# Turning the first batch's tokens by pairs of heads, loading its states second, and keeping two instead of four unsplit first tiles

## The chip, the cores and the metric

The kernel runs on one core of a Trainium2 chip. The metric is the time of one execution on the device in microseconds (us). An execution with a profile gives a trace; its span is somewhat shorter than its time, which also holds what lies around it.

## The reference

Eight batches of tokens `x` (8 heads, 512 tokens, 64 values a head) and of states (8 heads, 32 states, 64 values) read each other by softmax attention; both results go through one feed-forward layer. All inputs are double-precision numbers of which the kernel reads the words it needs.

```python
scores = scale * x @ state.T                  # (8, 8, 512, 32): tokens read states
a = softmax(scores, over states);  xread = a @ state
a2 = softmax(scale * state @ x.T, over tokens);  sread = a2 @ x
x_ = concat(xread, sread)                     # 8 * (512 + 32) rows of 512
h = x_ @ w_in                                 # 512 x 2048
g = h * clip(h + 3, 0, 6) / 6
out = g @ w_out                               # 2048 x 512
```

## The kernel before

**Stages.** The hidden layer's 2048 columns are 16 tiles of 128; a sweep is 8 of them. The units of work are: batches 0 to 7 with the first 8 tiles, the state rows of all batches with both halves, then batches 0 to 7 again with the other 8 tiles. A unit has 8 steps, one for each hidden tile. A step's first product makes `h` of a tile (in `ps_h`), ScalarE and VectorE make `g` of it, and two steps later its second products add `g @ w_out` into four accumulators (`acc0` to `acc3`, one for each 128 tokens).

**The states inside the weights.** For the token rows, `xread @ w_in` is computed as `a @ (state @ w_in)`: `wprime` multiplies the states of a batch (`stT`, turned) with tiles of `w_in` (through `all_heads`) and gives `wp`; the first product then multiplies `wp` with the turned softmax weights `aT`.

**Split numbers.** A single-precision product runs as slow passes on TensorE. So operands are split into a high part that TensorE takes in its fast format and the rest (`hi`, `lo`), and three fast products stand for one (`product`, `split`). The split costs a cast on ScalarE and a subtraction on VectorE for each tile. For the first tiles of batch 0 (`plain`) neither `wp` nor `g` nor `w_out` is split: the products run in single precision, with `a_first` as the weights. What those tiles' `w_out` needs in split form for later batches is made later (`late_halves`).

**The start.** `load_x(0, ...)` brings batch 0's tokens and `load_state(0, ...)` its states. VectorE copies the tokens into `xb`, TensorE turns them (`take_in`), and ScalarE copies the result into `xT` (which lies in `w_in3`). `tokens_by_rows` puts the turned states into block form (`apart`), multiplies them with `xT` (`scores`), makes the softmax with tokens in rows (maximum, difference, Exp, sum, reciprocal, product), turns the weights on TensorE and copies them into `a_first`. `scores_by_columns` makes the same scores with states in rows for `sread`. While TensorE has nothing, transposes of the identity keep it busy (the `idle` of `Plan.issue`). Later batches come turned by another way: 16 loads of 32x16x32 blocks each (`load_turned`) and transposes on VectorE, in two halves that each need one of three `raw` buffers.

**Weights.** `weight` loads a tile (or two) of double-precision words into a `raw` or `early` buffer, casts its upper words on ScalarE (`upper`, into `tops`) and joins them with the lower ones on VectorE (`join`).

**What sets the order.** The code adds operations with reads, writes, costs and due times to a `Plan`; a table of numbers, `RANKS`, one for each operation, gives their priority. `Plan.order` simulates five queues with the costs and takes, at each point, the operation with the lowest rank among those that can start soon. The resulting order is fixed in the program: each engine and SyncE's load queue run their rows strictly one after another. So a row that waits holds up all rows behind it on its engine.

```python
plain = lambda k, c: k == 0 and c == 0        # tiles 0 to 3 of batch 0
at(3, halves_of_first, 3.5)
```

## Time and profile before

| | |
|---|---|
| time, median of 3 runs | 647.61 us (646.58 to 649.05) |
| the profiled execution | 647.05 us |
| its span | 645.3 us |
| granted TensorE clock, mean | 1.0 |
| TensorE busy | 634.2 us (98%) |
| VectorE busy | 508.3 us (79%) |
| ScalarE busy | 324.8 us (50%) |
| GpSimd busy | 18.4 us (3%) |
| moved by DMA | 73.09 MB, mean 113 GB/s |

The times in the profile count from the start of the span. A row of the order of time has its start, its duration, the engine (PE is TensorE, PEld its weight loads, DVE VectorE, ACT ScalarE, SP SyncE; SPq is the issuing of loads), the line, the operation with its output and inputs, and how many equal ones were merged. A single-precision product counts as two records. Line numbers are those of the kernel before; in the changed kernel the same code stands some 10 to 33 lines further down.

### The profile page before, as it was taken

How to read it: one execution, taken by the hardware profiler on the slowest of the kernel's cores; microseconds unless marked ns; L12 is line 12 of the kernel's file. 1: busy time of each engine (PE TensorE's matmuls, PEld its weight loads, DVE VectorE, ACT ScalarE, POOL GpSimd, SP SyncE). 2: the span in 40 equal slices, each digit the busy share in tenths (PEclk: the TensorE clock that was granted, in tenths of full speed). 3: DMA queues.
4: the chain of work that ended last, by engine and by line, in shares of the span. 5: the costliest groups of instructions: out<-in, count | busy, mean ns of one | idle time of the engine just before them, and what ended most of it. 6: DMA issues, size and time to landing. Idle time of an engine off the chain costs nothing.

```text
span 645.3 us, 11398 instructions
## 1 busy us (share of the span) xinstructions
PE 634.2 (98%) x4422; PEld 515.2 (80%) x4422; DVE 508.3 (79%) x931; ACT 324.8 (50%) x585; POOL 18.4 (3%) x22
## 2 busy tenths in 40 slices
PE   7999999999999999999999999999999999999997
PEld 6446767777777868778899878898989898998996
DVE  5989778987979859878478769878887888798673
ACT  4848444555546444546346446455445454455431
POOL 0000000000000000000000000000000000000000
PEclk9999999999999999999999999999999999999999
DMA  9976696986839569344104032242424232413143
GB/s 296 247 195 184 133 201 101 261 170 165 190 71 234 122 192 215 87 78 145 21 1 135 1 103 70 40 100 34 102 35 99 33 89 25 112 21 60 15 81 70
DMA packets 148686, 73.09 MB, mean 113 GB/s; under 512 B 124696, under 2 KB 134424, under 8 KB 148504
## 3 DMA queue, kind: packets, MB, share of 16 engines
q1 hardware_dynamic: 144664, 64.23, 39.5%
q0 software_dynamic: 3824, 7.87, 8.4%
q8 instruction: 35, 0.57, 0.4%
q10 hardware_dynamic: 144, 0.26, 0.1%
q14 instruction: 19, 0.16, 0.1%
HBM read 42.45 MB, written 26.21 MB: 106 GB/s over the span
## 4 chain that ended last, share of the span: by engine, by line
PE 86%; DMA 5%; SPq 4%; DVE 2%; ACT 2%; issue 0%; DVEq 0%; ACTq 0%
PE ps_h L998 27%; PE acc L998 27%; PE acc L1110 24%; PE ps_s L614 3%; DMA early<-in_moe_w_out_dram 2%; PE ps_h L614 2%; PE acc L1281 1%; SPq L601 1%; DMA raw<-in_x_dram 1%; SPq L569 1%; DMA raw<-in_moe_w_out_dram 1%; DMA early<-in_moe_w_in_dram 1%; PE ps_h L955 1%; PE ps_h L1213 1%; ACT tops L472 1%; SPq L534 0%
## 5 line engine op out<-in xcount | busy, mean ns | idle before, releaser
L998 PE MATMUL acc<-w_out_hi,g_hi 128*128 128x512 f32 x288 | 114.9, 399 | 0.6 <-ACT g_hi L383 0.6
L998 PE MATMUL acc<-w_out_lo,g_hi 128*128 128x512 f32 x288 | 112.5, 391 | 0.2 <-DVE w_out_lo L506 0.2
L998 PE MATMUL acc<-w_out_hi,g_lo 128*128 128x512 f32 x288 | 112.2, 390 | 0.0
L1249 ACT ACTIVATE g<-ps_h,three 128x512 f32<-128x512 f32 (+1 forms) x80 | 51.2, 645 | 76.9 <-PE ps_h L998 64.7
L1110 PE MATMUL acc<-w_out_hi,tmp 128*128 128x256 f32 x360 | 89.0, 284 | 0.0
L998 PE MATMUL ps_h<-aT_hi,wp_hi 128*128 128x512 f32 (+1 forms) x224 | 81.3, 363 | 0.1
L998 PE MATMUL ps_h<-aT_lo,wp_hi 128*128 128x512 f32 (+1 forms) x224 | 80.8, 361 | 0.0
L998 PE MATMUL ps_h<-aT_hi,wp_lo 128*128 128x512 f32 (+1 forms) x224 | 80.4, 359 | 0.0
L1233 ACT ACTIVATE G<-ps_h,three 128x512 f32<-128x512 f32 x64 | 44.2, 691 | 68.4 <-PE ps_h L998 66.5
L1252 DVE SCALAR_TENSOR_TENSOR g<-g,ps_h 128x512 f32<-128x512 f32 (+1 forms) x80 | 50.0, 629 | 36.3 <-ACT g L1249 35.6
L998 PEld LDWEIGHTS acc<-w_out_hi,g_hi 128*128 128x128 f32 x288 | 54.1, 188 | 19.2 <-issue 7.2
L1110 PEld LDWEIGHTS acc<-w_out_hi,tmp 128*128 128x128 f32 x360 | 66.6, 192 | 3.0 <-issue 1.7
L1110 PE MATMUL acc<-w_out_hi,g_hi 128*128 128x256 f32 x240 | 68.2, 284 | 0.0
L1110 PE MATMUL acc<-w_out_lo,g_hi 128*128 128x256 f32 x240 | 67.9, 283 | 0.0
L1110 PE MATMUL acc<-w_out_hi,g_lo 128*128 128x256 f32 x240 | 67.9, 283 | 0.0
L998 PEld LDWEIGHTS acc<-w_out_hi,g_lo 128*128 128x128 f32 x288 | 54.1, 188 | 11.9 <-DVE g_lo L384 0.4
L998 PEld LDWEIGHTS acc<-w_out_lo,g_hi 128*128 128x128 f32 x288 | 54.1, 188 | 11.3 <-DVE w_out_lo L506 0.7
L1235 DVE SCALAR_TENSOR_TENSOR G<-G,ps_h 128x512 f32<-128x512 f32 x64 | 43.7, 686 | 20.8 <-ACT G L1233 20.1
L384 DVE TENSOR_TENSOR g_lo<-g,g_hi 128x512 fp32r<-128x512 f32 (+1 forms) x72 | 45.2, 641 | 10.7 <-ACT g_hi L383 9.0
L383 ACT CAST g_hi<-g 128x512 fp32r<-128x512 f32 (+1 forms) x72 | 40.8, 583 | 22.8 <-DVE g L1252 14.9
L1110 PE MATMUL acc<-w_out_lo,tmp 128*128 128x256 f32 x180 | 50.9, 283 | 0.0
L1110 PEld LDWEIGHTS acc<-w_out_hi,g_hi 128*128 128x128 f32 x240 | 45.9, 191 | 4.7 <-issue 2.5
(148 smaller groups left out, 1177.5 us busy)
## 6 DMA issues: line engine op xcount, KB each, us to landing
out_dram<-ot SPq DMA_DIRECT2D x8, 1024.0 KB, 5.2
out_dram<-ot POOLq DMA_DIRECT2D x15, 512.0 KB, 6.0
raw<-in_x_dram SPq DMA_DIRECT2D x112, 64.0 KB, 3.1
xb<-in_x_dram SPq DMA_DIRECT2D x28, 256.0 KB, 4.3
raw<-in_moe_w_out_dram SPq DMA_DIRECT2D x11, 511.8 KB, 4.0
raw<-in_moe_w_in_dram SPq DMA_DIRECT2D x8, 511.0 KB, 4.4
raw<-raw SPq DMA_DIRECT2D x112, 32.0 KB, 2.0
early<-in_moe_w_in_dram SPq DMA_DIRECT2D x3, 1023.0 KB, 9.3
```

Source lines behind the costliest of these rows:

```text
L383: first = S_(cost, rank, lambda: nc.scalar.copy(hi(), src()), reads, [writes[0]], after)
L384: V(cost, rank, lambda: nc.vector.tensor_tensor(lo(), src(), hi().bitcast(F32), op=ALU.subtract), [*reads, writes[0]], [writes[1]])
L472: nc.scalar.copy(out[..., 1], top)
L569: nc.sync.dma_start(x_tile(b, read)[:, :, j, :], x_v[b, j])
L601: nc.sync.dma_start(t[rows, i].rearrange("t (a c) -> t a c", c=NS), x[b, 4 * g + 2 * i + u, :, k * NS : (k + 1) * NS].rearrange("(a t) c - ...
L614: nc.tensor.matmul(out[u][cols, :], made["stT", b][rows, cols], moving(q)[rows], start=True, stop=True,)
L998: nc.tensor.matmul(ps, l, r, start=start and k == 0, stop=stop and k == n - 1)
L1110: nc.tensor.matmul(out, left(a, l), right(b, r), start=p == 0 and z == 0 and y == 0, stop=p == FPS // 2 - 1 and y == 2, skip_group_check=True)
L1233: S_(0.68, n - 1.5, lambda: nc.scalar.activation(g(), by_pass(), AF.Relu, bias=three, scale=-1.0 if turned_sign(FPS + i) else 1.0), [ps], ...
L1235: V(0.63, n - 1.5, lambda: nc.vector.scalar_tensor_tensor(g(), g(), 6.0, by_pass(), op0=ALU.min, op1=ALU.mult), [ps], [g_key])
L1249: in_turn["g", n] = S_(cost + 0.05, rank, lambda: nc.scalar.activation(g(), bank(ps)[:, :width], AF.Relu, bias=three, scale=-1.0 if turned ...
L1252: V(cost, rank, lambda: nc.vector.scalar_tensor_tensor(g(), g(), 6.0, bank(ps)[:, :width], op0=ALU.min, op1=ALU.mult), [ps], [g_key])
```

## The change

Six edits, all in the first microseconds but the last:

1. Batch 0's tokens are loaded in four pieces of two heads (256 KB), not two of four heads. The copies, transposes and scores go by these pieces: the scores of heads 0 to 3 fill one bank and those of heads 4 to 7 the other, where the banks were halves of the tokens before. Each bank's softmax is finished by itself, with a sum and a reciprocal of its own.
2. Batch 0's states are loaded by one transfer with rows of 512 bytes (two states in a partition) where there were two with rows of 256 bytes, and it is second in the queue. TensorE turns them by four products with columns of the identity instead of one transpose.
3. Two first tiles of batch 0 stay unsplit instead of four. Tiles 2 and 3 are split in all of `wp`, `g` and `w_out` like the later ones.
4. The unsplit `wp` lies in a `tmp` buffer, the scores' Exp in the second half of `w_in2`; the halves of the first weights (`halves_of_first`) are due two steps earlier.
5. Costs in the plan: VectorE's and ScalarE's are taken by 0.98, turning of tokens at 0.7 instead of 0.92.
6. `RANKS` is a new table of 2594 numbers, and with it the order of all engines changes to the end.

`split_by_queue` is added but nothing calls it.

```diff
-189 379 188 282 281 288 283 88 289 90 342 86 341 91 343 87 345 279 291 67 85 278 280 327 287 276 286 335 285 274 273
...
     def V(cost, rank, do, reads=(), writes=(), after=()):
-        return plan.add("V", cost, rank, do, reads, writes, after)
+        return plan.add("V", 0.98 * cost, rank, do, reads, writes, after)
...
-    plain = lambda k, c: k == 0 and c == 0
+    PLAIN = 2
+    plain = lambda k, f: k == 0 and f < PLAIN
...
-        if k < FPC:
+        if k < PLAIN:
             late_halves.append(halves)
...
-            for u in range(NG):
-                nc.sync.dma_start(raw[:, u, :], st_v[b, :, :, u, :])
+            nc.sync.dma_start(raw, state[b].rearrange("h (m k) d -> (h m) k d", k=NG))
...
-        for g in range(NG):
-            hs = slice(g * HG, (g + 1) * HG)
+        load_state(0, rank)
+        for q in range(NQ):
+            hs = slice(q * NG, (q + 1) * NG)
             def load(hs=hs):
                 nc.sync.dma_start(raw()[:, hs], x[0, hs].rearrange("h (p j) d -> p h j d", j=J))
-            Q(rank, 524.288, load, writes=[(*raw_key, g)], pieces=512, late=0.6)
-            if g == 0:
-                load_state(0, rank)
...
+            Q(rank + 0.1 * q, 262.144, load, writes=[(*raw_key, q)], pieces=256, late=0.5)
             V(0.37, rank, lambda hs=hs: nc.vector.tensor_copy(x_tile(0)[:, hs], raw()[:, hs]),
-              [(*raw_key, q // 2)], [(*key, "q", q)])
+              [(*raw_key, q)], [(*key, "q", q)])
...
-            T(0.25, rank, lambda: nc.tensor.transpose(
-                bank(st)[:, :P], made["st_raw", b].rearrange("p u d -> p (u d)"), ident),
-                [("st_raw", b)], [st], after)
+            def turn_first():
+                for u in range(NG):
+                    out = bank(st)[u * D : (u + 1) * D, :P].rearrange("p (q m k) -> p q m k", q=NQ, k=NG)
+                    for k in range(NG):
+                        nc.tensor.matmul(
+                            out[..., k], made["st_raw", b][:, k],
+                            ident.rearrange("p (q u m) -> p q u m", q=NQ, u=NG)[:, :, u], start=True, stop=True)
+            T(0.5, rank, turn_first, [("st_raw", b)], [st], after)
...
-        def scores(k):
-            out = bank(ps[k]).rearrange("p (j u q n) -> p j q u n", j=J // 2, u=NG, n=NS)
-            for j in range(J // 2):
-                for q in range(NQ):
-                    js = slice((k * J // 2 + j) * P, (k * J // 2 + j + 1) * P)
+        def scores(q):
+            out = bank(ps[q // 2]).rearrange("p (j u q n) -> p j q u n", j=J, u=NG, n=NS)
+            for j in range(J):
                     nc.tensor.matmul(
...
+        for e, bt_key in enumerate(bt_keys):
...
+            V(0.6, -6.21, lambda m1=m1, src=src: nc.vector.tensor_reduce(m1(), src(), axis=AX.X, op=ALU.max),
+              [ps[e]], [m1_key])
+            V(0.62, -6.21, lambda m1=m1, src=src, bt=bt: nc.vector.tensor_tensor(
+                bt(), src(), wide(m1()), op=ALU.subtract), [m1_key, ps[e]], [bt_key])
+            S_(0.62, -6.21, lambda bt=bt: nc.scalar.activation(bt(), bt(), AF.Exp, scale=SCALE), [], [bt_key])
+            V(0.6, -6.21, lambda s1=s1, bt=bt: nc.vector.tensor_reduce(s1(), bt(), axis=AX.X, op=ALU.add),
+              [bt_key], [s1_key])
+            V(0.1, -6.21, lambda s1=s1: nc.vector.tensor_scalar_add(s1(), s1(), 1e-9), [], [s1_key])
+            V(0.2, -6.21, lambda s1=s1: nc.vector.reciprocal(s1(), s1()), [], [s1_key])
+            V(0.62, -6.21, lambda s1=s1, bt=bt: nc.vector.tensor_tensor(bt(), bt(), wide(s1()), op=ALU.mult),
+              [s1_key], [bt_key])
...
-    at(3, halves_of_first, 3.5)
+    at(1, halves_of_first, 1.5)
```

What the new table and the new code make of the order is shown at two places. The first is SyncE's load queue from its first row. `ot` takes batch 0's tokens, `st_raw` states, `early` and `raw` weights, and `raw<-in_x_dram` are blocks of batch 1's tokens. Before:

```order
L581 DMA ot<-in_x_dram 128x4x256 x2
L527 DMA st_raw<-in_state_dram 128x1x64 x2
L459 DMA raw<-in_moe_w_out_dram 128x2047
L601 DMA raw<-in_x_dram 32x16x32
L459 DMA early_109<-in_moe_w_in_dram 128x4x511 x2
L459 DMA early_112<-in_moe_w_in_dram 128x4x1023
L459 DMA early_149<-in_moe_w_in_dram 128x4x1023
```

and further down, where the last weights of the first eight tiles of `w_in` follow:

```order
L534 DMA st_raw<-in_state_dram 32x4x32 x4
L601 DMA raw<-in_x_dram 32x16x32 x5
L459 DMA early_356<-in_moe_w_in_dram 128x4x1023
L1354 DMA s_361<-stT 128x128
L1350 DMA a0hi<-aT_hi 128x1024
```

Now the queue begins with

```order
L591 DMA ot<-in_x_dram 128x2x256
L536 DMA st_raw<-in_state_dram 128x128
L591 DMA ot<-in_x_dram 128x2x256 x2
L469 DMA early_105<-in_moe_w_in_dram 128x4x511
L591 DMA ot<-in_x_dram 128x2x256
L469 DMA early_105<-in_moe_w_in_dram 128x4x511
L469 DMA raw<-in_moe_w_out_dram 128x2047
L469 DMA early_127<-in_moe_w_in_dram 128x4x1023
```

and the place of batch 1's tokens is

```order
L469 DMA early_185<-in_moe_w_out_dram 128x2047
L469 DMA early_205<-in_moe_w_out_dram 128x2x2047
L469 DMA early_314<-in_moe_w_in_dram 128x4x1023
L1383 DMA a0hi<-aT_hi 128x1024
L607 DMA raw<-in_x_dram 32x16x32 x2
L1383 DMA a0lo<-aT_lo 128x1024
L607 DMA raw<-in_x_dram 32x16x32 x14
```

The states moved up behind the first quarter of tokens, `w_in`'s first two tiles stand ahead of all of `w_out`, the last quarter of tokens stands between them, and batch 1's tokens moved from between the weights to behind `w_in`'s eighth tile.

The second place is ScalarE at the start, from the first copy of turned tokens into `w_in` (that is `xT`); `tops` are casts of weights. Before:

```order
L710 COPY w_in_141<-acc_130 128x512
L710 COPY w_in_141<-acc_135 128x512
L710 COPY w_in_141<-acc_144 128x512
L472 CAST tops<-raw 128x512
L710 COPY w_in_141<-acc_155 128x512
L504 CAST w_out_hi_184<-raw 128x512
L472 CAST tops<-early_109 128x512 x2
L728 ACTIVATE tmp<-tmp 128x512
```

Now:

```order
L724 COPY w_in_147<-acc_129 128x512
L724 COPY w_in_147<-acc_141 128x512
L482 CAST tops<-early_105 128x512
L724 COPY w_in_147<-acc_152 128x512
L482 CAST tops<-early_105 128x512
L724 COPY w_in_147<-acc_180 128x512
L802 ACTIVATE w_in_195<-w_in_195 128x8x64
L482 CAST tops<-raw 128x512
```

The cast that stood ahead of the last copy was one of `w_out`'s first tile; now the third copy stands behind the cast of `w_in`'s first tile and the fourth behind that of its second, and the first half's Exp comes before `w_out`.

On TensorE the scores, one block of 16 products before, are two blocks of 8 around the transposes of the last quarter of tokens, and all 16 loads of batch 1's tokens must have been turned before its scores, as before.

More of the change, by code (lines that the diff above doesn't have):

```diff
@@ L373, in bank, with split_by_queue @@
         return get(key, lambda: pools.get(key[0], ps_acc).tile([P, 512], F32, name=key[0]))
+    def split_by_queue(rank, hi, lo, src, reads, writes, cost=0.62, after=()):
+        S_(cost, rank, lambda: nc.scalar.copy(hi(), src()), reads, [writes[0]], after)
+        S_(cost, rank, lambda: nc.scalar.mul(lo(), src(), -1.0), reads, [writes[1]])
+        first = plan.add("P", 1.25, rank, lambda: nc.gpsimd.dma_start(
+            lo(), src(), accum_op=ALU.add), reads, [writes[1]], (), 520.0, 128, 2.0)
+        plan.ops[first][4].add(first - 2)
     def split(rank, hi, lo, src, reads, writes, cost=0.62, negated=False, after=()):
@@ L537, in load_state @@
         if b < TURNED:
-            plan.add("Q", 0.9, rank, load, (), [key], after, 400.0)
+            plan.add("Q", 0.46, rank, load, (), [key], after, 90.0, 128, 0.6)
             return
@@ L617, in all_heads, with wp_32 @@
                 )
+    WP_32 = ("tmp", ("wp", 0))
+    def wp_32():
+        return get(WP_32, lambda: att.tile([P, NG, PLAIN * P], F32, name="tmp", bufs=8))
     def wp_key(k, c, f0, u, half):
@@ L658, in wprime @@
                 cost = 0.08 + 0.54 * n / CH
[L659 to L663 removed]
+                if plain(k, c * FPC + f0):
+                    S_(cost - 0.02, rank, lambda u=u, fs=fs, there=there: nc.scalar.copy(
+                        wp_32()[:, u, fs], there()), [bs[u]], [(*WP_32, f0, u)])
                     continue
@@ L761, in tokens_by_rows @@
             V(0.2, URGENT, put, [("stT", b)], [("apart", u)])
-        ps = [("ps_s", ("M", b, k)) for k in range(2)]
+        ps = [("ps_s", ("M", b, e)) for e in range(2)]
         half = lambda k: slice(k * S // 2, (k + 1) * S // 2)
-        def scores(k):
-            out = bank(ps[k]).rearrange("p (j u q n) -> p j q u n", j=J // 2, u=NG, n=NS)
-            for j in range(J // 2):
-                for q in range(NQ):
-                    js = slice((k * J // 2 + j) * P, (k * J // 2 + j + 1) * P)
-                    nc.tensor.matmul(
-                        out[:, j, q], xT(b, q)[:, js], apart[:, q],
-                        start=True, stop=True,
-                    )
@@ L774, in tokens_by_rows @@
-        for k in range(2):
-            scores_at[b] = T(1.85, rank(1), lambda k=k: scores(k),
-                             [("apart", u) for u in range(NG)]
-                             + [xT_key(b, q) for q in range(NQ)], [ps[k]], after(1))
-        bt_keys = [("tmp", ("bt", b, k)) for k in range(2)]
-        for k in range(2):
-            softmax_parts(b, k, rank, bt_keys[k], ps[k])
-        softmax_ends(b, rank, bt_keys)
-        for k, bt_key in enumerate(bt_keys):
+        bt_keys = [("w_in2", "a", "bt", e) for e in range(2)]
@@ new lines, in scores @@
+        def scores(q):
+            out = bank(ps[q // 2]).rearrange("p (j u q n) -> p j q u n", j=J, u=NG, n=NS)
+            for j in range(J):
+                nc.tensor.matmul(
+                    out[:, j, q % 2], xT(b, q)[:, j * P : (j + 1) * P], apart[:, q],
+                    start=True, stop=True,
+                )
+        for q in range(NQ):
+            scores_at[b] = T(0.93, rank(1) + 0.1 * q, lambda q=q: scores(q),
+                             [("apart", u) for u in range(NG)] + [xT_key(b, q)], [ps[q // 2]], after(1))
@@ L783, in tokens_by_rows, with turn @@
+        for k in range(2):
             back = (banks[k] if banks else "ps_s", ("B", b, k))
-            def turn(back=back, bt_key=bt_key):
+            def turn(back=back, k=k):
                 for g in range(NG):
                     for j in range(J // 2):
-                        cols = [slice((i * 2 + m) * P, (i * 2 + m + 1) * P) for i, m in ((g, j), (j, g))]
-                        nc.tensor.transpose(bank(back)[:, cols[0]], tmp(bt_key)[:, cols[1]], ident)
-            T(0.47, rank(4), turn, [bt_key], [back], after(4))
+                        nc.tensor.transpose(
+                            bank(back)[:, (2 * g + j) * P : (2 * g + j + 1) * P],
+                            first_weights()[:, (J // 2 * k + j) * NG + g].rearrange("p q n -> p (q n)"), ident)
+            T(0.47, rank(4), turn, bt_keys, [back], after(4))
```

42 lines of the change are left out of this document (23 added, 19 removed), and 202 rows, old and new, of the table RANKS.

## The prediction

> **What bounds the kernel now.** I read the page's busy table first, then the table of stages, and after it the start in order of time, engine by engine.
>
> ```profile
> span 645.3 us, 11398 instructions
> PE 634.2 (98%) x4422; PEld 515.2 (80%) x4422; DVE 508.3 (79%) x931; ACT 324.8 (50%) x585; POOL 18.4 (3%) x22
> 0.00:10.00 10.00, 6.54 (x35) 5.66 (x35) 3.27 (x10) 3.98 (x7) 0.95 (x7) 1.00 0.85 245
> 10.00:20.00 10.00, 8.87 (x102) 7.01 (x103) 9.01 (x16) 6.58 (x14) 0.00 (x0) 1.00 1.08 356
> 20.00:35.00 15.00, 14.16 (x70) 6.34 (x70) 12.45 (x24) 12.56 (x26) 0.00 (x0) 1.00 0.95 257
> 35.00:50.00 15.00, 14.84 (x68) 7.01 (x69) 12.92 (x24) 6.26 (x12) 0.00 (x0) 1.00 0.66 137
> 50.00:100.00 50.00, 49.48 (x387) 35.48 (x386) 40.89 (x77) 28.41 (x52) 0.00 (x0) 1.00 0.83 178
> 100.00:200.00 100.00, 99.30 (x692) 76.11 (x692) 86.68 (x158) 53.14 (x93) 0.00 (x0) 1.00 0.71 170
> ```
>
> The columns of a stage are its length, then busy time of PE, PEld, DVE, ACT and POOL, the granted clock, the DMA share and GB/s. TensorE is the bound: from 50 us on it is idle 0.5 us in 50 and 0.7 in 100. So a change pays in two ways only: less TensorE work, or an earlier start of the work that fills it. TensorE's own busy time is no help at the start, since 41 of its instructions there are transposes of the identity that keep it awake. I take the start of the feed-forward as the first L1213 product.
>
> ```profile
> 10.43 3.79 PE L770 MATMUL ps_s<-sread_t,w_in 128*128 128x64 f32 x32 [1.71 <-ACT w_in L710]
> 21.27 1.98 PE L1213 MATMUL ps_h<-w_in,wp 128*128 128x512 f32 x4
> 23.19 0.66 PE L614 MATMUL ps_s<-w_in,stT 64*32 64x256 f32 x16
> 25.60 5.56 PE L1281 MATMUL acc<-raw,g 128*128 128x512 f32 x12
> 31.09 0.66 PE L614 MATMUL ps_s<-w_in,stT 64*32 64x256 f32 x16
> 35.16 1.98 PE L1213 MATMUL ps_h<-w_in,wp 128*128 128x512 f32 x4 [0.92 <-ACT wp L662]
> 43.26 1.09 PE L614 MATMUL ps_s<-tmp,stT 64*32 64x512 f32 x16
> 6.20 1.74 ACT L710 COPY w_in<-acc 128x512 f32<-128x512 f32 x3 [3.96 <-PE acc L705]
> 9.17 0.76 ACT L472 CAST tops<-raw 128x512 f16<-128x512 bf16 x1 [1.23 <-DMA raw<-in_moe_w_out_dram]
> 9.80 0.58 ACT L710 COPY w_in<-acc 128x512 f32<-128x512 f32 x1
> 7.43 0.30 PE L684 MATMUL ps_s<-ident,st_raw 128*128 128x128 f32 x1 [0.15 <-DMA st_raw<-in_state_dram]
> 4.57 0.76 DVE L587 COPY xb<-ot 128x512 f32<-128x512 f32 x2 [2.60 <-DMA ot<-in_x_dram]
> 6.14 0.76 DVE L587 COPY xb<-ot 128x512 f32<-128x512 f32 x2 [0.81 <-DMA ot<-in_x_dram]
> 13.87 0.68 DVE L726 TENSOR_TENSOR tmp<-ps_s,m 128x512 f32<-128x512 f32 x1
> 14.47 0.68 DVE L724 TENSOR_REDUCE m<-ps_s 128x16 f32<-128x512 f32 x1
> 18.14 0.35 DVE L738 RECIPROCAL s<-s 128x32 f32<-128x32 f32 x1
> 18.53 1.29 DVE L741 TENSOR_TENSOR tmp<-tmp,s 128x512 f32<-128x512 f32 x2
> ```
>
> (Start, duration, what, and in brackets the idle time before it and what ended that.) The start is a chain: tokens land, are copied, transposed and copied again; the last copy stands on ScalarE behind a cast that waits for w_out's first tile, and so the scores start only at 10.43. They run as one block of 3.79 us before the two softmax halves can finish, and 21.27 follows.
>
> **The start, step by step.** Transfers come in as a train. These are issue times of SyncE's queue and, from the table of DMA issues asked for each of them, what they took to land.
>
> ```profile
> 0.74 0.44 SPq L581 DMA_DIRECT2D ot<-in_x_dram  x1
> ot<-in_x_dram SPq DMA_DIRECT2D x1, 512.0 KB, 3.8
> 3.19 0.47 SPq L459 DMA_DIRECT2D raw<-in_moe_w_out_dram  x1
> raw<-in_moe_w_out_dram SPq DMA_DIRECT2D x1, 511.8 KB, 5.9
> 4.17 0.62 SPq L459 DMA_DIRECT2D early<-in_moe_w_in_dram  x1
> early<-in_moe_w_in_dram SPq DMA_DIRECT2D x1, 511.0 KB, 6.7
> 4.84 0.88 SPq L459 DMA_DIRECT2D early<-in_moe_w_in_dram  x1
> early<-in_moe_w_in_dram SPq DMA_DIRECT2D x1, 511.0 KB, 7.5
> ```
>
> The first 512 KB land at 4.5, w_out's 512 KB at 9.1, w_in's at 10.9 and 12.3: 1.5 us for each 512 KB of w_in, and 0.8 for 256 KB. The new queue is tokens, states, tokens, tokens, w_in 0, tokens, w_in 1, w_out 0. A first quarter of tokens lands 0.8 before 4.5, at 3.7. The states are 64 KB in 128 rows; between 0.2 us (their bytes at the tokens' rate) and 1.25 (what the two old loads of 256-byte rows took at most, from the tokens' second half at 6.14 to the transpose of the states at 7.43) I take 0.4, by rows: a quarter of tokens is 256 rows in 0.8. So: states 4.1, tokens 4.9 and 5.7, w_in 0 at 7.2, last tokens 8.0, w_in 1 at 9.5, w_out 0 at 11.2. The last tokens land later than now (6.14), and that is a loss which the new order hides: only a quarter of the scores is left for them.
>
> But ScalarE's new order puts the fourth copy of tokens behind the cast of w_in 1, as it now stands behind that of w_out. So the gate is 9.5: cast to 10.2 (0.65), copy to 10.75 (0.58), the last four score products 0.95 (a quarter of 3.79), to 11.7, where now the scores end at 14.2. The first half's maxima and differences lie before that. Behind it on VectorE, at 0.6 each from the rows' spacing: maximum 12.3, difference 13.0 with a small sum between, reciprocal 13.3, w_out's join 13.9, the first half's product 14.5, the second half's sum 15.1 (its Exp lies beside the join), small sum and reciprocal 15.6, last product 16.2 to 16.5. From the end of that product (19.82 now) to the first feed-forward product are 1.45 us now, for turning, four copies and the wait between. **So the start moves from 21.27 to 17.9: -3.4 us.** Its bounds: 17.1, if w_in 1 lands 0.8 sooner, and 20.7, if it lands as late as now (12.3). The four-piece tokens cost two more issues, the states one less and three more small products on TensorE; all lie in its idle time there (3.5 us of the first 10). The Trainium skill ("DMA: Bandwidth & Descriptors", Specifications) puts the least row for full rate at 512 B; by that the states cost the lower bound, 0.2, and the sum would be 0.2 better; no row here shows loads of that size.
>
> **The two unsplit tiles.** A single-precision first product takes 1.92 us a tile (21.27 to 23.19), its four second products 3.66 (12 records from 25.60 to 31.09, 8 of them a tile); split ones take:
>
> ```profile
> 69.46 1.36 PE ps_h L998 x6
> 70.82 2.72 PE acc L998 x12
> ```
>
> These are pieces of the chain that ended last. 5.58 against 4.08 is 1.5 a tile, **-3.0 us** for two, all of it on the engine that binds. The price is on others: for two tiles two casts of g (ScalarE, 0.6 each), two g_lo (0.6 each) and two wp_lo (0.35 each) on VectorE, 1.2 and 1.9 us. From 20 to 35 us these engines have 2.4 and 2.5 us free, so it just fits; if not, it is TensorE that waits.
>
> **What the faster start meets.** I carried the new order on by hand with the same durations. The next limit is the train of weights, 8.6 MB up to w_in 6 and 7: at the spacings above (3.1 for a megabyte, 1.6 for half a one, 1 for the states between) w_in 2,3 land at 14, w_out 1 and 2 by 17.3, w_in 4,5 at 20.3, w_out 3 to 5 by 26, w_in 6,7 at 28.5 to 29. Now that last load is issued only at 27.11, since loads of batch 1's tokens, waiting for buffers, stand ahead of it, and it costs the 0.92 us before 35.16:
>
> ```profile
> 27.11 5.46 DMA early<-in_moe_w_in_dram
> ```
>
> With the tokens of batch 1 moved behind these weights it lands some 4 us sooner; TensorE wants it at 31.2 and its two joins end at 30.5: that wait goes, **-0.9**. ScalarE is then full from 17 to 33 us, and by my count the third tile's g is split 0.5 us late: **+0.5**. Next late are batch 1's tokens. Their second half needs the buffer of w_out 2, free at 32.0; the same eight loads now:
>
> ```profile
> 31.70 6.69 SPq L601 DMA_DIRECT2D raw<-in_x_dram  x8
> 41.16 1.29 DVE L696 STREAM_TRANSPOSE tmp<-raw 128x512 f32<-128x512 f32 x2
> ```
>
> Their 9.5 us from issue to transposes, 1.3 for these, would end at 42.8; TensorE is there at 41.6 (now 43.26). Between 0, if the loads come faster with fewer others in flight, and 1.2 I take the middle, **+0.6**. For other waits of the new order after 50 us, where all rows are reordered: between -1.2 (all of today's, 0.5 and 0.7) and some 3 us; I take **+0.5**.
>
> **Sum:** -3.4 - 3.0 - 0.9 + 0.5 + 0.6 + 0.5 = -5.7 us. Against the profiled execution (647.05, of which 645.3 span and 1.75 around it) that is 641.35; its time is 0.56 under the median of the runs, 647.61, so I forecast 641.9.
>
> **The rivals.**
>
> *Weights late.* w_in 1 lands at 12.3 as now; everything behind ScalarE's cast shifts by 2.8. Against it: now 64 KB of 128-byte rows and 512 KB of w_out stand ahead of it that no longer do. Gain 2.9: 644.7.
>
> *The clock.* If that gap grows further, TensorE idles long enough to lose its clock. In this trace the granted clock is 1.00 in every stage of the start, with no idle stretch above 1.7 us; the fillers fall from 41 to 32. The Trainium skill ("TensorE: Matmul & The Clock Gate", HAM oscillation) wants no idle gap over about 3.4 us; by that rule, and the trace cannot contradict it, my longest gap, about 1.6 before the turning of the weights, is safe. For one stretch at half clock the last scores (0.95) and turns (1.26) would take 2.2 us more, on top of 2.8 for the late landing: 646.9.
>
> *Given back at the batch starts (the other side).* Each batch's first products wait for its attention, which goes through VectorE. The two waits of this kind now, the longest of all after 50 us and batch 1's first product:
>
> ```profile
> PE acc L998 <- ACT g_hi L383: 0.6, 1, 0.6
> 61.94 0.47 PE L998 MATMUL ps_h<-aT_hi,ot 128*128 128x512 f32 x1 [0.29 <-DVE wp_lo L384]
> ```
>
> VectorE is 82 to 87% busy in these stages (40.89 of 50, 86.68 of 100). The new order may leave such a wait at each of the seven later batches. At 1 us each the gain is gone (7 less today's 0.9, against 6.2, the gain without my last +0.5); above 1.5 each the kernel is slower by more than 0.5%. At 1.6 each: 11.2 less 0.9 less 6.2, 4.1 more: 651.7. Against it: the loads of later batches are released by TensorE's steps, so that they move along with an earlier start, and batch 1 gets 18.7 us of TensorE work between its scores and its first product in the new order, where its attention has 17.6 now (from 44.35, the end of its scores, to 61.94).
>
> *The change doesn't do it.* The start is set by the softmax chain and not by its gate: the first product comes at 20.5, and only the tiles and the wait at 35.16 pay: -0.8 in place of -3.4, 644.5.
>
> **How the numbers follow.** A measurement of this kernel tells 0.5%, 3.2 us, from no change. My forecast, a gain of 4 to 8 us, has 0.66; weights late 0.10; the change doesn't do it 0.06; the clock 0.03; given back at the batch starts 0.15, of which 0.08 slower and 0.07 within 0.5%. Faster by over 0.5%, under 644.4: 0.66 and half of the two cases just above it (0.08), 0.74; within 0.5%: 0.08 + 0.03 + 0.07 = 0.18; slower 0.08. The range is 638.5 (start at 17.1, 0.8; tokens without a wait, 0.6; today's waits after 50 us gone, 1.7; 3.1 better) to 646.5, which takes in late weights and half of the waits given back; that leaves out some 0.18.
>
> **What would show it.** Right: the first L1246 product at 17 to 19 us; the fourth token copy on ScalarE right behind a cast that waited for w_in; scores in two blocks of eight; 16 records of L1314 where L1281 had 32; no wait of over 0.5 us at wp for tiles 6 and 7; batch 1's scores (L620 from tmp) at 41 to 43. Wrong: a first product after 20.5, TensorE waiting for batch 1's tokens over 2 us, or waits of a microsecond at the batch starts after 55.

## The result, and the profile after

The changed kernel took 654.6 us (median of four runs, 652.8 to 656.7); the kernel before took 648.1 in the same comparison. The ratio is 1.0103, with a 95% interval of 1.0067 to 1.0140: slower by one per cent, where 641.9 was forecast. In the profiled execution (656.7 us, the longest of the four) the span is 654.9 us, 9.6 more than in the profiled one before; the medians differ by 6.5.

The busy table of the page after, and its stages (same columns as in the prediction):

```profile
span 654.9 us, 11423 instructions
PE 638.0 (97%) x4432; PEld 522.2 (80%) x4432; DVE 509.3 (78%) x937; ACT 325.9 (50%) x587; POOL 18.4 (3%) x22
```

```profile
10.00:20.00 10.00, 10.00 (x82) 7.50 (x82) 6.50 (x14) 5.01 (x11) 0.00 (x0) 1.00 1.05 384
50.00:100.00 50.00, 46.28 (x376) 32.99 (x375) 43.68 (x82) 28.38 (x50) 0.00 (x0) 1.00 0.75 157
100.00:200.00 100.00, 96.46 (x682) 74.43 (x681) 84.14 (x152) 50.14 (x86) 0.00 (x0) 1.00 0.68 156
200.00:300.00 100.00, 97.38 (x632) 74.50 (x631) 76.11 (x135) 47.55 (x83) 0.00 (x0) 0.98 0.61 147
```

TensorE is still the bound, but it now idles 3.7 us in 50 to 100 and 3.5 in 100 to 200, where it had idled 0.5 and 0.7. And in 10 to 20 it is busy all the time (8.87 before), with fewer instructions (82 for 102): each takes longer. TensorE in order of time shows it:

```profile
1.57 2.18 PE L1523 MATMUL ps_h<-ident 128*128 128x128 f32 x9 [1.57 <-POOL ident masks.py:199]
...
6.47 1.97 PE L719 MATMUL acc<-ident,xb 128*128 128x128 f32 x8 [1.02 <-DVE xb L593]
8.23 3.51 PE L783 MATMUL ps_s<-sread_t,w_in 128*128 128x64 f32 x16
...
23.12 3.25 PE L1246 MATMUL ps_h<-w_in,tmp 128*128 128x512 f32 x7
...
46.59 1.09 PE L620 MATMUL ps_s<-tmp,stT 64*32 64x512 f32 x16
```

Sixteen records of score products take 3.51 us, 0.22 each; before, 32 took 3.79, 0.12 each. TensorE runs at half rate from the first product to about 20 us, with no idle time after 6.47, and the column of the granted clock says 1.00 there all the same: at the start only the spacing of the records tells. It tells of the kernel before too. The same transpose of the identity took 0.23 us there at first and 0.14 later, and its records change their spacing at 6.5 us:

```profile
1.57 3.03 PE L1490 MATMUL ps_h<-ident 128*128 128x128 f32 x13 [1.57 <-POOL ident masks.py:199]
...
8.01 0.71 PE L1490 MATMUL ps_h<-ident 128*128 128x128 f32 x5
```

So ScalarE's fourth copy of tokens no longer waits for a weight's cast but for TensorE:

```profile
10.45 0.76 ACT L482 CAST tops<-early 128x512 f16<-128x512 bf16 x1 [0.99 <-DMA early<-in_moe_w_in_dram]
12.64 0.59 ACT L724 COPY w_in<-acc 128x512 f32<-128x512 f32 x1 [1.43 <-PE acc L719]
```

The first feed-forward product comes at 23.12, 1.85 later than before. The other loss is in the waits of TensorE after 22 us (in total, times, longest; the same view of before had 0.9, 0.6, 0.3 and 0.2):

```profile
PE acc L1031 <- ACT g_hi L392: 3.8, 2, 2.6
PE ps_h L1006 <- DVE g L1285: 2.1, 1, 2.1
PE ps_h L988 <- DMA raw<-raw: 1.5, 1, 1.5
PE ps_s L925 <- ACT tmp L891: 1.0, 2, 0.6
PE ps_h L1031 <- DVE wp_lo L393: 0.9, 1, 0.9
PE ps_h L1031 <- DVE ot L393: 0.4, 1, 0.4
PE acc L1031 <- DVE g_lo L393: 0.2, 1, 0.2
```

The three longest have one pattern, a step that stands one place too late in a row that is worked off strictly in order. SyncE's queue, ScalarE and TensorE after, in order of time:

```profile
113.00 1.60 SPq L469 DMA_DIRECT2D raw<-in_moe_w_in_dram  x1
114.64 0.59 SPq L960 DMA_DIRECT2D raw<-raw  x1
...
152.83 0.76 ACT L482 CAST tops<-raw 128x512 f16<-128x512 bf16 x1 [6.24 <-DMA raw<-in_moe_w_out_dram]
...
206.21 0.77 ACT L480 ACTIVATE tops<-raw 128x512 f16<-128x512 bf16 x1 [5.18 <-DMA raw<-in_moe_w_in_dram]
207.51 1.12 ACT L392 CAST g_hi<-g 128x512 fp32r<-128x512 f32 x2
208.17 0.77 PE L1031 MATMUL acc<-w_out_hi,g_hi 128*128 128x512 f32 x1 [2.62 <-ACT g_hi L392]
```

and the stage behind the last of them:

```profile
208.00:212.00 4.00, 3.83 (x9) 2.75 (x9) 3.64 (x9) 3.18 (x7) 0.00 (x0) 0.57 1.07 223
```

At 113 the small move that TensorE needs (`raw<-raw`) is issued behind a weight load that takes 1.60 to issue. At 153 and 206 the cast of a weight tile stands ahead of the activation or the cast that TensorE needs, and ScalarE waits 6.24 and 5.18 us for the transfer. After the last pause the granted clock is 0.57 for 4 us, another 1.7 us.

The account of the 9.6 us: start +1.85, listed waits +7.9 (9.9 for 2.0), lower clock +1.7, two split tiles -2.4 (an estimate by the spacing of the records: unsplit products -10.4, 36 split ones +8.0); the rest, +0.5, is small waits that the view doesn't list.

### The profile page after: what moved, and what is told of

Its sections match the earlier page's. It is cut to its first block, busy times and chain, and to the rows that moved or that the text cites. A ratio compares the mean times of both kernels' runs of the same rounds, so it can differ in the third digit from the quotient of the medians.

```text
span 654.9 us, 11423 instructions
## 1 busy us (share of the span) xinstructions
PE 638.0 (97%) x4432; PEld 522.2 (80%) x4432; DVE 509.3 (78%) x937; ACT 325.9 (50%) x587; POOL 18.4 (3%) x22
## 4 chain that ended last, share of the span: by engine, by line
PE 84%; DMA 5%; DVE 5%; SPq 3%; ACT 2%; issue 1%; DVEq 0%; ACTq 0%
PE ps_h L1031 26%; PE acc L1031 25%; PE acc L1143 23%; PE ps_s L620 3%; SPq L607 2%; DMA raw<-in_moe_w_in_dram 2%; PE ps_h L620 2%; PE ps_s L783 1%; DVE g L1285 1%; DMA st_raw<-in_state_dram 1%; DMA raw<-in_moe_w_out_dram 1%; ACT g L1282 1%; DVE g_lo L393 1%; PE acc L1314 1%; DMA ot<-in_x_dram 1%
## 5 line engine op out<-in xcount | busy, mean ns | idle before, releaser
L1031 PE MATMUL acc<-w_out_hi,g_hi 128*128 128x512 f32 x296 | 119.1, 402 | 3.8 <-ACT g_hi L392 3.8
L1031 PE MATMUL acc<-w_out_lo,g_hi 128*128 128x512 f32 x296 | 116.2, 392 | 0.0
L1031 PE MATMUL acc<-w_out_hi,g_lo 128*128 128x512 f32 x296 | 116.0, 392 | 0.2 <-DVE g_lo L393 0.2
L1031 PE MATMUL ps_h<-aT_hi,wp_hi 128*128 128x512 f32 (+1 forms) x228 | 83.4, 366 | 1.6 <-DVE wp_lo L393 0.9
L1031 PEld LDWEIGHTS acc<-w_out_hi,g_hi 128*128 128x128 f32 x296 | 56.0, 189 | 23.6 <-issue 7.2
L1031 PEld LDWEIGHTS acc<-w_out_hi,g_lo 128*128 128x128 f32 x296 | 56.0, 189 | 13.0 <-DVE g_lo L393 1.1
L1031 PEld LDWEIGHTS acc<-w_out_lo,g_hi 128*128 128x128 f32 x296 | 56.1, 190 | 10.9 <-issue 0.5
L393 DVE TENSOR_TENSOR g_lo<-g,g_hi 128x512 fp32r<-128x512 f32 (+1 forms) x74 | 47.0, 643 | 12.1 <-ACT g_hi L392 10.5
L392 ACT CAST g_hi<-G 128x512 fp32r<-128x512 f32 (+1 forms) x64 | 37.9, 606 | 27.9 <-PE acc L1143 19.8
L1031 PEld LDWEIGHTS ps_h<-aT_hi,wp_hi 128*128 128x128 f32 x228 | 43.1, 189 | 9.9 <-DVE wp_lo L393 1.3
```

The costliest lines, as they stand in the source:

```text
L392: first = S_(cost, rank, lambda: nc.scalar.copy(hi(), src()), reads, [writes[0]], after)
L393: V(cost, rank, lambda: nc.vector.tensor_tensor(lo(), src(), hi().bitcast(F32), op=ALU.subtract), [*reads, writes[0]], [writes[1]])
L1031: nc.tensor.matmul(ps, l, r, start=start and k == 0, stop=stop and k == n - 1)
```

## The experiments

Two theories. **Clock:** the loss comes from the half rate at the start. **Order:** it comes from the new order of rows after batch 0. The rival to both is the one of the prediction, that an earlier start is given back at the batch starts whatever the order. Ratios are against the kernel before in the same session (medians 648.67, 649.05, 649.27 and 648.89).

### 1. Four more fillers at the first wait (changed kernel)

```diff
-for _ in range(int((self.start[n] - last - 0.25) / (0.22 if last < 8.0 else 0.13))):
+for _ in range(int((self.start[n] - last - 0.25) / (0.22 if last < 8.0 else 0.13)) + 4 * (last == 2.0)):
```

> The changed kernel with 13 filler products ahead of the first transposes, not 9, so that TensorE has no pause from 1.6 to about 4.6 us, as the kernel before had. Theory 1 (the late first product comes from TensorE running at half rate up to 20.4 us, because too little dense work stood at the very start): the 128x128 products fall from a mean of 421 ns to some 275 ns by about 7 us, the first L1246 product starts near 19.5 us and not at 23.1, and the time falls by 3 to 4 us, to about 651. Rival 1 (the rate has nothing to do with the fillers; the 64-column scores keep it down): the half rate stays to 20 us, the start is 23 to 24 and the time 655 or a little over.

Measured 650.57 us (648.73 to 654.03), ratio 1.0035 (1.0013 to 1.0056). TensorE in order of time, and one stage:

```profile
7.50 1.97 PE L783 MATMUL ps_s<-sread_t,w_in 128*128 128x64 f32 x16
...
19.17 3.68 PE L1246 MATMUL ps_h<-w_in,tmp 128*128 128x512 f32 x8
```

```profile
202.00:206.00 4.00, 4.00 (x17) 1.99 (x23) 3.75 (x10) 2.71 (x6) 0.00 (x0) 0.63 1.28 220
```

Full rate comes at 5.1 us, before the first scores, the start is at 19.17, and some two thirds of the loss are gone (two fifths, if it is measured by run 12, below); the listed waits are still 7.4 us, and the clock still falls after the pause at 200. So the rate at the start is one cause and not the only one.

### 2. Four fewer fillers in the kernel before

```diff
+            ... + -4 * (last == 2.0)):
```

> The kernel before with 9 fillers ahead of its first transposes, not 13. Theory 1: it too stays at half rate well past 6.5 us, its scores take some 420 ns a record instead of 275, its first L1246 product falls from 21.3 to about 24, and the time rises by 2 to 3 us to about 650.5. Rival 1: full rate from about 6.5 us as before, start 21 to 21.5, time 648 as before.

Measured 647.73 us (647.19 to 650.58), ratio 0.9979 (0.9960 to 0.9998). TensorE was at half rate to about 10 us, 3 us longer than in the kernel before, and at full rate in the scores; the first product came on time:

```profile
10.47 3.79 PE L770 MATMUL ps_s<-sread_t,w_in 128*128 128x64 f32 x32 [0.53 <-ACT w_in L710]
...
21.30 1.98 PE L1213 MATMUL ps_h<-w_in,wp 128*128 128x512 f32 x4
```

Half rate up to 10 is thus hidden in the old start: TensorE still waits 0.53 us (1.71 before) for ScalarE's last copy, and its scores begin at 10.47 (10.43 before). Whether half rate that lasts longer is hidden too, this run does not show; 8 does.

### 3. The changed start with the later order of before

```diff
-        for n in ...                         # the row is found from RANKS as priorities
+        for n in ranks:                      # RANKS is the row itself: the changed kernel's first
+            ...                              # 176 steps, then before's row
```

> The changed kernel up to its 176th step (all of the start, through the loads of batch 1's tokens), and from there the row of steps of the kernel before. Theory 2 (the waits after 50 us belong to the new order's later rows, where loads of weights stand behind loads of tokens): TensorE's idle time after 50 us falls from 10.4 us to about 2, while the start stays at 23.1; the time is about 646. Rival 2 (those waits are an echo of the late start, whatever the order): idle time of 8 us or more stays, and the time is 652 to 655.

Measured 649.68 us (647.32 to 651.92), ratio 1.0008 (0.9990 to 1.0026): the whole loss is gone, though it has nine fillers as the changed kernel has. A start at 23.1 and a time of about 646 had been expected; in its profiled execution (647.32, the shortest of ten) full rate came at 4.9 us. From 100 to 300 us TensorE idles 1.0 us (6.2 in the changed kernel). But it does not win either, though its start is 1.84 us earlier than before's, its two tiles 2.4 cheaper and the wait at 35 (0.9) gone. Where those 5.1 us went can be read here, since both kernels have the same rows from batch 1's scores on. VectorE's and TensorE's of this kernel:

```profile
19.43 3.68 PE L1246 MATMUL ps_h<-w_in,tmp 128*128 128x512 f32 x8
...
41.14 1.30 DVE L710 STREAM_TRANSPOSE tmp<-raw 128x512 f32<-128x512 f32 x2
...
41.54 2.00 PE L620 MATMUL ps_s<-tmp,stT 64*32 64x512 f32 x16
...
58.28 1.04 PE L925 MATMUL ps_s<-ident,tmp 128*128 128x128 f32 x8
...
60.24 0.68 DVE L393 TENSOR_TENSOR wp_lo<-ps_h,wp_hi 128x512 fp32r<-128x512 f32 x1
...
61.07 0.47 PE L1031 MATMUL ps_h<-aT_hi,ot 128*128 128x512 f32 x1 [1.75 <-DVE wp_lo L393]
```

and the two of before that the prediction does not show:

```profile
60.62 1.03 PE L892 MATMUL ps_s<-ident,tmp 128*128 128x128 f32 x8
...
61.11 0.68 DVE L384 TENSOR_TENSOR wp_lo<-ps_h,wp_hi 128x512 fp32r<-128x512 f32 x1
```

The last turns of batch 1's tokens start at 41.14 here and at 41.16 before: its tokens are ready no earlier. Their last block lands at 40.16 (40.66 before), and VectorE has a `g_lo` to do first. TensorE is at their scores at 41.54, 1.7 us before the old time, and they take 2.00 in place of 1.09 since VectorE is still turning the tokens. Behind the scores VectorE runs without a gap up to `wp_lo` in both kernels, and is there 0.87 earlier (60.24 for 61.11). TensorE, 2.34 ahead at the transposes (58.28 for 60.62), then waits 1.75 and is 0.87 ahead. The rest is lost by 105 us, most of it at 92 to 96, where products of the attention (L620) stand; of the wait of 0.87 at 102 the kernel before has 0.6 too. So in this kernel the gain went into batch 1's attention: its tokens and VectorE set the time there, not TensorE.

### 4. Both

```diff
+            ... + 4 * (last == 2.0)):                                 # on top of 3
```

> Both edits at once: 13 fillers, and the row of before from the 176th step on. Theories 1 and 2 together: start near 19.5, little idle time after 50 us, about 642.5, faster than both kernels. If rival 1 holds, 646; if rival 2 holds, 649 to 651; if both rivals hold, 654.

Measured 647.5 us (646.44 to 652.30), ratio 0.9987 (0.9961 to 1.0012): the kernel before again, where 642.5 had been forecast. The profiled execution was the longest one, and shows that 13 fillers don't assure full rate:

```profile
8.51 3.52 PE L783 MATMUL ps_s<-sread_t,w_in 128*128 128x64 f32 x16
...
23.50 3.69 PE L1246 MATMUL ps_h<-w_in,tmp 128*128 128x512 f32 x8
```

### 5 and 6. No first fillers, and many plain ones (both with the row of 3)

```diff
+            ... + -9 * (last == 2.0)):                                # 5
+            ... + {9: 10, 13: 4, 17: 4}.get(n, 0)):                    # 6
-        nc.tensor.transpose(awake, ident, ident)
+        nc.tensor.matmul(awake, t, t, start=True, stop=True)           # 6; t is cleared tops, then ident
```

> As the kernel with the later order of before, but with none of the 9 fillers ahead of the first transposes. The profiles so far show the rate at the start as a draw: 9 fillers gave half rate to 20 us once and full rate at 6.3 us once, 13 fillers gave each once. Theory 1, restated (whether an execution finds enough dense products early decides when full rate comes, and with the changed start, whose steps wait for TensorE, a late full rate costs about 4 us of the whole): without fillers every execution is at half rate to about 20 us, the first L1246 product starts at 23 to 24, and all times lie near 651, none near 647. Rival (the draw has nothing to do with the fillers): times as spread as before, 647 to 652, median 649.7.

> The same kernel with 6 products of a cleared tile that start before the identity is there, 13 identity fillers behind them, 3 more in the pause before the second tokens' transposes and 3 in the next pause: dense work from about 0.7 us to 8 us. Theory 1, restated: every execution reaches full rate by about 7 us, the first L1246 product starts at 19 to 19.5, times are all near 647 with none above 650. Rival: half rate still comes in a part of the executions, and the median stays at 648 to 650.

Without fillers: 650.99 us (646.89 to 652.2), ratio 1.0034 (1.0014 to 1.0055). Eight of ten runs lie from 650.29 to 652.2, but two lie at 646.89 and 648.41, where none was expected; the profiled one is the shortest, and has full rate from about 8 us and its start at 19.28. With many plain products: 652.52 us (651.13 to 653.33), ratio 1.0052 (1.0034 to 1.0070). Its spread is the least of all, 2.2 us in 7 runs, and full rate comes at about 6 us; but plain single-precision fillers count twice, and those ahead of the start are in the way:

```profile
17.56 3.17 PE L1523 MATMUL ps_h<-ident 128*128 128x128 f32 x26
...
23.00 1.45 PE L1246 MATMUL ps_h<-w_in,tmp 128*128 128x512 f32 x3
```

So it missed its forecast by its own cost, and says of the clock only that runs then agree better.

### 7. Three pairs of steps moved in the changed kernel's row, with 13 fillers

```diff
-473 452 481 474 784 491 454 475 ...
+473 452 481 474 454 784 491 475 ...
-607 ... 657 659 590 666 ... 608 ... 758 661 609 721 759 610 662 761 699 757 611 ...
+590 607 ... 657 659 666 ... 758 661 721 759 608 662 761 757 609 610 699 611 ...
-882 871 883 923 ... 872 878 876 865 887 921 877 940 ...
+882 883 923 ... 878 876 865 887 871 921 877 872 940 ...
```

The first line puts the small move ahead of the weight load (113 us). The second puts a load of tokens ahead of a load of `w_out`, and the second and third put the cast and the join of a weight tile behind the activation, `g_hi` and `g_lo` that TensorE waits for (153 and 206 us).

> The changed kernel with 13 first fillers and its own order, but for six steps moved by one to three places: the 16th move of raw to raw ahead of the w_in load behind which it stood (near 113 us), the eighth load of tokens ahead of a w_out load and that tile's cast and join behind the g_hi and g_lo next to them (near 147), and a w_in tile's cast and join behind the g_hi and g_lo next to them (near 206). Theory 2 (these waits are made by single steps at the head of a queue): against the kernel with 13 fillers alone the waits of 0.8, 1.0 and 1.9 us go, and with the last of them the half rate at 202 to 207 us (about 2 us): 645 to 647, that is 4 to 5 us less than 650.6. Rival 2 (the new order is short of time there as a whole): the waits turn up at the next step, and the time is 649 or more.

Measured 648.2 us (646.51 to 651.32), ratio 0.9993 (0.9973 to 1.0012), between the forecast of 645 to 647 and the rival's 649. The start and TensorE's waits:

```profile
20.03 3.68 PE L1246 MATMUL ps_h<-w_in,tmp 128*128 128x512 f32 x8
```

```profile
PE ps_h L1031 <- DVE ot L393: 1.3, 2, 0.7
PE acc L1031 <- DVE g_lo L393: 1.3, 2, 1.1
PE acc L1031 <- ACT g_hi L392: 1.2, 1, 1.2
PE ps_h L1031 <- DVE wp_lo L393: 0.8, 1, 0.8
...
PE ps_h L988 <- DMA raw<-raw: 0.2, 1, 0.2
...
```

Six steps of 2594 take the three waits out (0.2 is left of the first, 0.65 at another step near the third), and the lower clock behind the third. The rest is at 50 to 66 us, around batch 1's attention.

### 8. The kernel before without its 13 first fillers

```diff
+            ... + -13 * (last == 2.0)):
```

> The kernel before with none of its 13 fillers ahead of the first transposes, so that it is at half rate through its start in every execution. Theory 1, restated (before's start waits for the loads of its tokens and for the softmax, and TensorE has time to spare even at half rate): first L1213 product at 21.3 to 22, time 648 to 649, no change. Rival (half rate costs before as much as after): first product near 25, time 652.

Measured 647.65 us (646.25 to 649.43), ratio 0.9981 (0.9966 to 0.9996). In the profiled execution, the longest, the half rate lasts to about 22 us and now the old start is late too, where 21.3 to 22 had been expected:

```profile
10.27 7.09 PE L770 MATMUL ps_s<-sread_t,w_in 128*128 128x64 f32 x32 [0.20 <-ACT w_in L710]
...
24.71 1.55 PE L1213 MATMUL ps_h<-w_in,wp 128*128 128x512 f32 x3 [0.20 <-ACT w_in L794]
```

Its first product is 3.4 us later than in the profile of the kernel before and its span 2.4 longer (647.7 for 645.3): by these two profiles 1.0 us of such a delay is taken back later. How the other nine executions started is not known.

The intervals of 2 and 8 end just under 1, and the mean granted clock, which is on record for every execution, goes with that. Of the 108 executions of the kernel before in the four sessions, 67 have a mean of 0.995 or less, and their median is 649.8 us; the other 41 have 648.2. None of the 20 executions of 2 and 8 is under 0.999. So the kernel before, with 13 first fillers, loses its clock for some us in more than half of its executions, and with 9 or none in none of those measured. At which place it loses it is not shown, since its one profile has no such loss; and a half rate that lasts from the first product on, as in 8's profile, is not in this mean (0.999 there).

### 9 to 11. Warming up earlier

```diff
+            ... + {9: 7, 13: 4, 17: 4}.get(n, 0)):                     # one product of cleared tops first, then transposes
```

9 has the row of 3, 10 that row with eight more steps of VectorE and ScalarE moved, 11 the row of 7.

> The kernel with the later order of before, and more fillers of the cheap kind: one product of a cleared tile ahead of the identity, 15 identity fillers, and 3 more in each of the two pauses that the transposes of the tokens leave. The many fillers tried first were plain products, which the profile shows as two passes each where a transpose takes one; they kept every execution together (651.1 to 653.3) but held the start back to 23.0 at full rate. Theory 1, restated: full rate by about 6 to 8 us in every execution, start 19.2 to 20, all times within 2 us of each other near 647. Rival: two groups of times again, 647 and 651.

> The same, with eight steps moved by a few places on VectorE and ScalarE where TensorE still waits at 49 to 51, 59 and 93 us: batch 1's second maxima and exps ahead of its first softmax, one lower half of W' ahead of two joins, and batch 2's exps ahead of a cast of weights that comes in late. If each wait is one step at the head of a queue, 2 to 3 us less than without the moves, about 644.5, faster than before by 0.6%. If the stretch is short of VectorE time, the waits come back behind the moved steps, and the time is as without them.

> The changed kernel's own order with the three swaps, and the same cheap fillers. If the start's draw and those three waits are all that the change lost, 646 to 647 with no time over 649; the waits at 50 to 65 us stay. If the draw stays, two groups at 647 and 651.

Measured 648.46 (646.93 to 650.38), ratio 0.9987 (0.9972 to 1.0002); 648.81 (648.05 to 654.06), ratio 1.0000 (0.9982 to 1.0018); 648.74 (647.62 to 651.88), ratio 0.9997 (0.9982 to 1.0013). None beats the kernel before, and none comes to what was forecast (647, 644.5, 646 to 647). The profiled execution of 9 shows full rate early, at 5 us, and then its loss again (order of time, and one stage):

```profile
7.39 1.97 PE L783 MATMUL ps_s<-sread_t,w_in 128*128 128x64 f32 x16
...
11.17 0.66 PE L719 MATMUL acc<-ident,xb 128*128 128x128 f32 x4 [1.47 <-DVE xb L593]
...
21.82 3.68 PE L1246 MATMUL ps_h<-w_in,tmp 128*128 128x512 f32 x8
```

```profile
12.00:18.00 6.00, 6.00 (x66) 4.26 (x65) 4.43 (x9) 3.10 (x9) 0.00 (x0) 0.50 1.04 398
```

A pause of 1.47 us for the last tokens is followed by 6 us at a granted clock of 0.50, and the start is back at 21.82. The profiled executions of 10 and 11 (the longest of their twelve) show the same, and longer. Full rate comes at 4.2 us in both, is lost at 11 and is back at 21; the starts are at 23.36 and 23.63. A stage of 11:

```profile
12.00:20.00 8.00, 8.00 (x73) 5.50 (x72) 5.62 (x12) 4.56 (x11) 0.00 (x0) 0.50 1.06 386
```

Their mean granted clock is 0.994 (9) and 0.992 (10 and 11); of the 12 executions of each, 2, 2 and 1 have a mean of 0.995 or less. So early fillers bring full rate early, and in some executions it does not last. In 10 the waits that were moved away came up at other places (`L620<-g` 1.1, `w_out_lo` 0.8).

### 12. The changed kernel again

> The changed kernel, unaltered, to see whether its own start is a draw. Theory 1, restated: times in two groups some 4 us apart (about 650.5 and 654.5), since with 9 fillers one profile of the same start showed half rate to 20 us and another full rate at 6 us; the profiled run shows a start of 19.5 or of 23 by its group. Rival (its start is always the late one): all near 654.5.

Nothing changed. Measured 653.41 us (649.58 to 655.41), ratio 1.0058 (1.0035 to 1.0080). The eight times fall into no two groups 4 us apart. Its profiled execution (652.3) starts at 22.31, with half rate to between 18 and 19; the wait at 113 is 0.13, that at 153 2.1, that at 204 1.1. So in these two executions the places of the waits are the same, and the sizes of two of them are not.

### 13. Three more moves, and 14. the moves alone

13 adds to 7 three of VectorE's lower halves moved ahead; 14 is 7 with nine fillers again.

```diff
-181 233 259 232 ... 274 194 197 294 299 365 292 198 300 301
+181 233 259 232 ... 274 194 294 299 300 197 365 292 198 301
...
-            ... + 4 * (last == 2.0)):                                 # 14 alone
```

> The kernel with the three swaps and 13 first fillers (648.2 us), with three lower halves on VectorE moved two to four places ahead: one of W' near 56 us, one of W' near 95, one of g near 122, where TensorE still waits 0.84, 0.65 and 1.06 us. Theory 2 (the new order's waits are each a single step that stands too late in a queue): those three waits go, gaps after the start fall from 5.9 to some 3.5 us, time 645.5 to 646.5, faster than before by 0.4 to 0.5%. Rival 2 (VectorE is short of time in these stretches): the waits turn up at the steps that were passed, and the time stays at 648.

> The three swaps alone, with the 9 first fillers of the changed kernel: the fourth corner beside the changed kernel (654 us), 13 fillers alone (650.6) and both (648.2). If the swaps' gain does not depend on the start: 654 less 2.4 to 5, that is 649.5 to 651.5. If the waits at 113, 147 and 206 us are an echo of a late start: no gain, 653 to 654.

13 measured 649.17 us (647.48 to 652.21), ratio 1.0008 (0.9992 to 1.0023): no gain over 7. Its aims became small (0.84, 0.65 and 1.06 us are now 0.92 at another step, 0.22 and 0.15), but two pauses close together (0.92 before 57.13 and 1.42 before 59.65) cost the clock, in this stage:

```profile
60.00:62.00 2.00, 2.00 (x5) 1.31 (x5) 2.00 (x4) 0.33 (x2) 0.00 (x0) 0.50 1.27 264
```

14 measured 651.64 us (649.84 to 653.13), ratio 1.0042 (1.0023 to 1.0061), with half rate to about 21 us and the start at 23.75. The three waits are gone there too, so they are no echo of a late start. With that the two causes stand as a square:

| | row as changed | six steps moved |
|---|---|---|
| 9 fillers | 1.0103 (1.0067 to 1.0140), again 1.0058 (1.0035 to 1.0080) | 1.0042 (1.0023 to 1.0061) |
| 13 fillers | 1.0035 (1.0013 to 1.0056) | 0.9993 (0.9973 to 1.0012) |

Each mend takes back some 0.2 to 0.7%, both together all of it, and nothing beyond it. With the other mend in place each is clear of noise; alone, each is so only against the first of the two measurements of the changed kernel. No kernel with the change beats the one before; the two that stand lowest by ratio (2 and 8) are the one before with fewer fillers.

## Why the prediction was wrong, point by point

**The start (-3.4; measured +1.85).** This step failed, and by something that it had priced as a rival with 0.03. It costed TensorE's part of the chain by durations at full rate, and TensorE stayed at half rate to 20 us. "The granted clock is 1.00 in every stage of the start" was no evidence: the column reads 1.00 in both cases. What the trace before did show, and I didn't use, is the spacing: 0.23 us a filler at first, 0.14 later, and 0.12 a score product. The weights did come early (w_in 1 at 10.4, 0.9 over the 9.5 of the sum). At full rate the chain runs in the order that was worked out, and the first product comes at 19.0 to 20.0 in 1, 3, 5, 7 and 13: -1.2 to -2.3, within the bounds of 17.1 to 20.7 but short of the -3.4. In 1, where it is 19.2 for 17.9, 0.9 is the later w_in 1 (10.45), and 0.3 lies behind VectorE's last product. That the fillers fall from 41 to 32 was noted and then not priced.

**The two tiles (-3.0; measured -2.4).** Right in mechanism, 0.6 too large by the estimate above. VectorE and ScalarE did have room for the split: TensorE has no wait from 23 to 50 us, so the third tile's +0.5 did not come.

**The wait at 35 (-0.9).** Right: it is gone.

**Batch 1's tokens (+0.6).** In the changed kernel no wait is seen, since it starts 5 us later than forecast (its scores come 23.5 us after the start, 23.7 forecast). Where the start is early, in 3, the step is right, at 0.9 in place of 0.6; what it left out is VectorE's unbroken chain behind the tokens. It passes their time on to batch 1's first product, so that of the 2.6 us that TensorE could have been ahead there (1.75 waited, 0.87 left) two thirds are given back.

**Other waits after 50 us (+0.5, bounds -1.2 to +3; measured +8.8, and 1.7 for the clock).** TensorE's listed waits there are 9.9 us for 1.1. This is the term that was mis-sized most, and the range fell with it. I took it from today's waits, as if a new order of 2594 steps would wait as rarely as the old one. The new rows behind 60 us would have shown it: a weight load ahead of a small move that TensorE needs, casts of landing weights ahead of `g_hi`. The step did not use them.

**The rivals.** "Given back at the batch starts" (651.7, slower with 0.08) came nearest in time, but the large waits lie behind weight loads and not at the batch starts; its mechanism is what limits kernel 3. "The change doesn't do it" was wrong at full rate. "The clock" was right in kind and wrong in cause: I looked for an idle stretch, and in the changed kernel's start there was none over 1.6 us. The other rival, late weights, did not come by itself: w_in 1 landed 0.9 late, not 2.8.

**What would show it wrong** was named: a first product after 20.5, and waits of a microsecond after 55. Both came. The low end of the range, 638.5, is 0.3 under what its own terms give (641.9 less 3.1 is 638.8); that changes nothing here.

**Still open:** what decides in which execution full rate comes early. With nine fillers it came at 4.9 us (3), 10 (2) or 18 to 21 (after, 12, 14); with 13 at 5 to 7 (before, 1, 7, 13) or 21 (4); with none at 8 (5) or 22 (8). What decides whether it lasts is open as well. Also the waits at 50 to 66 us that 7 leaves: 13 tried to mend them and did not.

## What to carry to other kernels

Where engines work rows off strictly in order, look in a new order for every step that waits for a transfer, and for what the bounding engine needs behind it: moving six steps of 2594 took back 0.2 to 0.6% here. An earlier start is worth only as much as the next transfers come earlier with it; follow it to the first point where they don't. At a kernel's start read TensorE's rate off the spacing of equal products, and see how often it differs between executions before costing a chain by its fast durations. Where only one execution has a profile, look at the mean granted clock of the others.

## What the runs showed of the hardware that was not expected

**Half rate without idle time.** In the changed kernel TensorE had no idle time from 6.47 us on and stayed at 0.22 us a product to about 20 us; the same start ran at full rate from 4.9 us in kernel 3 (0.12 a score product). The Trainium skill ("TensorE: Matmul & The Clock Gate", Part 1, What's actually happening) gives about 3.4 us of sustained work for full rate. Kernel 3 agrees, with 3.3 us from its first product to full rate (1.57 to 4.9); the changed kernel does not, with some 14 us of work without a pause. The same page (Part 4: PE-mode transpose) says that transposes don't count as busy in the same way. The changed kernel's work is transposes up to 8.2 us, but from there to 15.8 mostly score products, which are none, and the half rate stayed; kernel 6 with plain products had the least spread, and kernels 1 and 3 came to full rate on transposes. So no run here shows that the kind of work decides.

**The clock sometimes falls after short pauses.** Pauses of 2.62 us (after, at 208), 1.94 (1, at 200), 1.47 (9, at 11), 1.42 (10, at 11) and 0.92 with 1.42 (13, at 57 to 60) were followed by a granted clock of 0.50 to 0.63 for 2 to 8 us, and 1.81 (11, at 9) by 0.50 from 11 us on; 2.08 (after, at 155) and the same 1.81 (7, at 11) were not. So the length of a pause alone does not decide. The prediction took 1.6 as safe by the page's rule (HAM oscillation) that only gaps over about 3.4 us count; by these rows shorter pauses can be followed by half the clock too.

**Small states in 512-byte rows.** They landed at 3.66, 0.17 us behind the first tokens; the 0.2 by the Trainium skill ("DMA: Bandwidth & Descriptors", Specifications) was nearer than the 0.4 that I took by rows. But that is not all that this place in the queue cost: the second quarter of tokens landed at 5.96, 2.3 behind the states where 0.8 was reckoned, and the loads behind it kept 0.5 to 1.0 us of that delay (w_in 0 at 8.17 for 7.2). No run here shows what held them.
